# Clustered attention and a channel MLP on one core: block transposes moved from TensorE to VectorE and DMA gathers

## The chip, the cores and the metric

The kernel runs on 1 core of one Trainium2 chip. The metric is the time of one execution on the device, in microseconds (us). Engines are named as in the profile: PE is TensorE, DVE is VectorE, ACT is ScalarE, POOL is GpSimd, SP is the engine whose queue issues nearly all DMAs.

## The reference, cut to what matters

```python
# q, k, v: (4 batches, 8 heads, 768 tokens, 64), centroids: (8, 16, 64)
q_assign = argmax(q_n @ c_n.T); k_assign = argmax(k_n @ c_n.T)      # q_n, k_n, c_n: rows divided by their norms
mask = q_assign[:, :, :, None] == k_assign[:, :, None, :]
scores = where(mask, 0.125 * q @ k.T, -1e9)
attn = softmax(scores);  x = (attn @ v) laid out as (4, 768, 512)
u = x + (x.T @ U @ V).T             # U: (768, 32), V: (32, 768), mixing over tokens
out = u + relu(u @ w_ch1) @ w_ch2   # (512, 2048), (2048, 512)
```

The argmax does not change when a token's similarities are all scaled, so q and k are not normalised in the kernel; only the centroids are.

## The kernel before

**Attention.** The work is cut into 16 pairs of heads (`i`, 4 to a batch). A pair takes 12 score tiles of 128 keys by 2 times 384 queries (`scores`, L474 and L476), their exponentials on ACT (`pr`, L479), their running sum on POOL (`T`, L489) and the products with v in two bursts (`values`, L497, tile `o_ps`). Before the exponentials it needs the largest score of each query: 24 matmuls into PSUM banks (`rowmax`, L450, tile `ps_max`), each read by a DVE reduction (L452). These banks come from a pool of four, `work`, which most other PSUM tiles of the stage share.

**Clusters.** The mask is part of the score matmuls: one-hot rows of the clusters are placed among the rows of q and k (`X1[...][64:96]`), scaled by 2^60. `sims` multiplies tokens with centroids and ACT scales the result by the centroids' norms (L343). `largest` turns the similarities with three PE transposes (L350, tile `ps_simT`), so that tokens lie on partitions. Five DVE operations (L354 to L366) find the first largest cluster and write one-hots. `clusters_T` turns those with six bf16 PE transposes (L375, tile `ps_oh`), ACT scales them (L377), and four DMAs put them in place.

**Mix.** At the end of each batch `mix_u`, `mix_sum` and `mix_v` compute u from x. u goes to DRAM (`u_scr`).

**MLP.** Batch 0 is multiplied in two halves of 384 tokens with 16 steps each (`gemm1`, `gemm2`); meanwhile the weights of batches 1 to 3 are prepared in blocks (`recover`, `combine`, `split_high`, `split_low`) and stored to DRAM (`store_block`, `store_sum`, tensors `wc`). Batches 1 to 3 use a two-level scheme of seven block products instead of eight ("sevens": `seven1`, `seven2`), 16 steps of seven products a batch, with weights fetched from `wc` on SP's queue (`fetch_w1`, `fetch_w2`). They need u with channels on partitions: `fetch_half` reads 384 tokens of u into `st`, `turn_half` turns them with 12 PE transposes (L766) and four ACT copies (L767). `u_sums` (L779, on DVE) and `u_halves` then prepare the operands.

**Order.** The program is one straight list. Every call is put on it by `at(time, ...)`: a unit of time is one score tile in attention (12 a pair), one step in batch 0's MLP, and four sevens products behind it. The tables `times`, `mixes`, `stages` and numbers in the loops set it, the list is sorted, and each engine runs its instructions strictly in that order, SP its DMAs too.

Of the kernel before, what the change touches and what calls it, by code (L numbers as in the profile page):

```python
# [35 lines left out]
ALU = mybir.AluOpType  # L36
# [17 lines left out]
GV = 6  # L54
BIG = float(2.0 ** 60)
# [16 lines left out]
    "place_ones":      (-14.55, -12.25,  -6.11,   None,   None, -20.84),
    "load_v":          ( -19.2,  -5.08,  -7.21,   None, -22.04,  -9.26),
    "rowmax":          (-14.88, -14.94,  -14.8, -12.52,  -8.11, -11.77),
    "rowmax_T":        ( -3.08,  -3.31,  -3.73,  -3.18,   0.25,  -2.19),
    "rowmax_place":    ( -2.26,  -2.27,   -2.6,   0.84,    2.2,  -0.15),
    "scores":          (     0,  -0.97,  -0.37,  -0.47,   0.82,   0.95),
    "weights":         (  1.45,  -0.22,   0.44,   2.06,   3.14,   1.67),
    "values":          (  1.31,   1.51,   0.02,   1.05,   3.05,   1.39),
    "sums":            ( 14.31,  14.69,  13.43,  14.01,  15.51,  15.47),  # L80
    "sums_T":          ( 16.16,  15.81,   14.3,  15.86,  17.06,  16.44),
    "normalise0":      ( 18.83,  16.88,  14.88,  19.57,  20.85,  21.01),
    "normalise1":      ( 21.59,  17.72,  15.28,   26.3,  23.84,  20.15),
    "largest":         (-23.05, -22.46, -20.21,   None,   None, -21.05),
    "clusters":        ( -21.3, -22.24, -20.12,   None,   None, -18.18),
# [4 lines left out]
    "mix_u":    ( 18.88,  18.35,  18.48,  16.57),  # L90
    "mix_sum":  ( 19.11,   19.1,  19.15,  17.65),
    "mix_v":    (  20.5,   20.4,  20.68,  18.42),
# [5 lines left out]
    "g0":   ( 35.66,  38.22,  42.54,  52.94),  # L98
    "g1":   (-26.11, -21.73,  -20.5, -18.29),
    "g2":   (  -2.6,  -1.45,  -0.45,  -0.02,   0.0,   0.53),  # L100
# [3 lines left out]
spots = [0.66, -0.06, 1.8, 2.25, 1.26, 2.09, 2.97, 3, 3.49, 3.81, 4.58, 5.03]  # L104
# [13 lines left out]
def clustered_attention_moe(ctx: ExitStack, tc: tile.TileContext, qk, v, cen, moe_U, moe_V, w1, w2, out):  # L118
# [25 lines left out]
    u_scr = [dram.tile([P, NT, DM], F32, name=f"u_scr{b}") for b in range(B)]  # L144
# [89 lines left out]
    for c in range(C):  # L234
        nc.gpsimd.memset(rank[:, c:c + 1], float(C - c))
    ident_b = one.tile([P, P], BF16, name="ident_b")
    osc = one.tile([P, 1], F32, name="osc")
    obi = one.tile([P, 1], F32, name="obi")
    sel = late.tile([P, 32], F32, name="sel")

    rep = late.tile([P, 96], F32, name="rep")
    onehot = [one.tile([P, NT, 4, 32], BF16, name=f"oh_{i}") for i in range(2)]
    ones = one.tile([2 * NT, P], F32R, name="ones")

    def constants(k):
        if k == 0:
            nc.gpsimd.memset(ones.bitcast(F32), 1.0)
            nc.gpsimd.memset(onehot[0], 0.0)
            make_identity(nc, ident_b)
            for k in range(4):  # L250
                nc.gpsimd.memset(osc[32 * k:32 * k + 32], (1.0, BIG)[k % 2])
                nc.gpsimd.memset(obi[32 * k:32 * k + 32], (0.0, -BIG)[k % 2])
        else:
            nc.gpsimd.memset(onehot[1], 0.0)
# [14 lines left out]
    def table(f):  # L269

        nc.scalar.activation(warm, rank[:, 0:1], f)
# [4 lines left out]
    def turn_centroids(p):  # L276
# [59 lines left out]
    def sims(i):  # L336
# [5 lines left out]
        sm = live["sims", i] = sb.tile([P, HS], F32, name="sims", bufs=1)  # L342
        nc.scalar.mul(sm, ps[:, 0:HS], c_rn[:, i % NP:i % NP + 1])  # L343

    def largest(i):

        ps = work("ps_simT")
        sm = live.pop(("sims", i))
# [3 lines left out]
        eq = live["eq", i] = ps[:, 0:HS].rearrange("p (g c) -> p g c", c=C)  # L352
        mx = sb.tile([P, NG4], F32, name="mx")
        nc.vector.reduce_max(mx, eq, axis=AX.X)  # L354
# [812 lines left out]
```

## Time and profile before

| | |
|---|---|
| time, median of 3 runs | 981.08 us (980.56 to 981.95) |
| profiled execution | 982.48 us, its span 980.70 us |
| busy in the span | PE 946.5, DVE 701.1, ACT 472.5, POOL 611.7 us |
| stages in the span (first instructions of each) | start 0, first score tile 31.9, batch 0's MLP about 482, sevens about 611 |

The time of an execution holds the span and what lies around it, here 1.78 us. The busy time of an engine is the union of its instructions; those of PE are pipelined, so a matmul's own duration is longer than the time until the next can start. Where a row below tells of two instructions that follow each other on PE, the difference of their starts is what the first one cost.

### The profile page before, as it was taken

The numbers are of one execution on the slowest core, as the hardware profiler recorded it, in microseconds if no ns is written. First come the engines' busy times: TensorE is split into PE (matmuls) and PEld (weight loads), VectorE is DVE, ScalarE is ACT, GpSimd is POOL, SyncE is SP. The second block draws the span as 40 slices with busy tenths as digits, with TensorE's granted clock in tenths as the row PEclk, the third lists the DMA queues.
The fourth block names the chain that finished last, engine by engine and source line by source line (L and its number), as shares of the span: only waits on it lengthen the run. The fifth ranks groups of instructions, "written<-read, shape, count | busy, mean of one in ns | idle before, by whom it ended". The sixth has DMA issues, their size and how long they took to land.

```text
span 980.7 us, 15364 instructions
## 1 busy us (share of the span) xinstructions
PE 946.5 (97%) x5368; PEld 776.7 (79%) x5368; DVE 701.1 (71%) x1300; ACT 472.5 (48%) x837; POOL 611.7 (62%) x459
## 2 busy tenths in 40 slices
PE   6899999999999999989999999999999999999997
PEld 3566666676667666655788998999999999999997
DVE  5797777877787776686877525856588665986776
ACT  4454555565565554466556554544345333353330
POOL 5456586788778886774255876744286542865433
PEclk9799999999999999999999999999999999999999
DMA  7755454755656663536599896787668686677644
GB/s 182 188 142 130 119 151 119 212 153 146 163 156 185 160 153 76 178 103 203 171 304 342 277 351 263 252 331 264 239 223 302 259 309 258 223 281 276 240 140 150
DMA packets 76158, 205.28 MB, mean 209 GB/s; under 512 B 8561, under 2 KB 42865, under 8 KB 71217
## 3 DMA queue, kind: packets, MB, share of 16 engines
q1 hardware_dynamic: 75552, 203.42, 64.7%
q8 instruction: 42, 0.69, 0.3%
q10 hardware_dynamic: 528, 0.89, 0.3%
q14 instruction: 36, 0.29, 0.1%
HBM read 131.07 MB, written 41.94 MB: 176 GB/s over the span
## 4 chain that ended last, share of the span: by engine, by line
PE 81%; DVE 9%; DMA 4%; ACT 3%; issue 2%; POOL 1%; SPq 0%; DVEq 0%; ACTq 0%; POOLq 0%
PE o_ps L497 13%; PE ps_max L450 8%; PE st L474 6%; PE st L476 6%; PE ps_p L825 3%; PE ps_p L824 3%; PE ps_p L823 3%; PE ps_q L899 3%; PE ps_q L824 3%; PE ps_q L825 3%; PE ps_q L823 3%; PE ps_q L901 3%; PE ps_q L900 3%; PE ps_p L899 2%; PE ps_p L901 2%; PE ps_p L900 2%
## 5 line engine op out<-in xcount | busy, mean ns | idle before, releaser
L489 POOL TENSOR_TENSOR T<-T,pr 128x768 f32<-128x768 f32 x120 | 226.3, 1886 | 47.4 <-ACT pr L479 20.9
L452 DVE TENSOR_REDUCE m<-ps_max 128x1 f32<-128x384 f32 x384 | 195.3, 547 | 84.1 <-PE ps_max L450 82.6
L479 ACT ACTIVATE pr<-st 128x768 f32<-128x768 f32 x192 | 154.9, 813 | 85.9 <-PE st L476 58.6
L497 PE MATMUL o_ps<-pr,vt 128*64 128x384 f32 x768 | 133.5, 498 | 0.1
L450 PE MATMUL ps_max<-arena 128*128 128x384 f32 x384 | 127.4, 382 | 6.5 <-DVE oh L366 2.5
L474 PE MATMUL st<-arena 128*128 128x384 f32 x384 | 105.7, 356 | 1.8 <-ACT pr L479 1.8
L450 PEld LDWEIGHTS ps_max<-arena 128*128 128x128 f32 x384 | 71.2, 194 | 44.9 <-issue 22.0
L497 PEld LDWEIGHTS o_ps<-pr,vt 128*64 128x64 f32 x768 | 53.1, 139 | 67.5 <-issue 61.4
L476 PE MATMUL st<-arena 97*128 97x384 f32 x384 | 100.2, 342 | 3.6 <-issue 1.9
L489 POOL TENSOR_TENSOR T<-pr 128x768 f32<-128x768 f32 x30 | 56.6, 1886 | 63.8 <-ACT pr L479 63.8
L474 PEld LDWEIGHTS st<-arena 128*128 128x128 f32 x384 | 66.7, 191 | 17.0 <-issue 9.9
L476 PEld LDWEIGHTS st<-arena 97*128 97x128 f32 x384 | 70.8, 191 | 5.6 <-issue 4.1
L501 ACT COPY os<-o_ps 128x384 f32<-128x384 f32 x32 | 15.4, 480 | 106.0 <-PE o_ps L497 106.0
L824 PE MATMUL ps_p<-arena,w 128*128 128x384 f32 x186 | 62.2, 334 | 0.0
L823 PE MATMUL ps_p<-arena,w 128*128 128x384 f32 x186 | 62.2, 334 | 0.0
L825 PE MATMUL ps_p<-arena,w 128*128 128x384 f32 x186 | 62.2, 334 | 0.0
L823 PE MATMUL ps_q<-arena,w 128*128 128x384 f32 x150 | 50.1, 334 | 0.0
L824 PE MATMUL ps_q<-arena,w 128*128 128x384 f32 x150 | 50.1, 334 | 0.0
L825 PE MATMUL ps_q<-arena,w 128*128 128x384 f32 x150 | 50.1, 334 | 0.0
L390 POOL TENSOR_TENSOR arena<-R,arena 128x768 fp32r<-128x768 f32 x18 | 34.3, 1908 | 13.8 <-ACT arena L385 8.2
L824 PEld LDWEIGHTS ps_p<-arena,w 128*128 128x128 f32 x186 | 34.9, 188 | 0.1
L823 PEld LDWEIGHTS ps_p<-arena,w 128*128 128x128 f32 x186 | 34.9, 188 | 0.1
(538 smaller groups left out, 2387.4 us busy)
## 6 DMA issues: line engine op xcount, KB each, us to landing
w<-wc SPq DMA_DIRECT2D x24, 1024.0 KB
w<-wc SPq DMA_DIRECT2D x24, 768.0 KB
arena<-wc SPq DMA_DIRECT2D x20, 768.0 KB
rw<-in_w SPq DMA_DIRECT2D x27, 512.0 KB
R<-in_qk SPq DMA_DIRECT2D x32, 384.0 KB
arena<-arena SPq DMA_DIRECT2D x32, 384.0 KB
arena<-arena SPq DMA_DIRECT2D x64, 192.0 KB
wc<-f SPq DMA_DIRECT2D x46, 256.0 KB
```

The lines of the kernel that those rows point to most:

```text
L450: nc.tensor.matmul(ps[:, 0:HS], x1[:, 0, g // 2, g % 2, t * P:(t + 1) * P], x1[:, 1, h, g % 2, :], start=True, stop=True)
L452: nc.vector.reduce_max(live["m2", i][:, h, u:u + 1], ps[:, 0:HS], axis=AX.X)
L474: nc.tensor.matmul(st[:, j, 0:HS], x1[:, 1, hk, j, ks], x1[:, 0, h, j, :], start=True, stop=False)
L476: nc.tensor.matmul(st[:, j, 0:HS], x2[0:97, 1, hk, j, ks], x2[0:97, 0, h, j, :], start=False, stop=True)
L479: nc.scalar.activation(pr, st[:, :, 0:HS], AF.Exp, scale=SCALE)
L489: eng.tensor_add(T, live["p", i, h, 0] if c == 1 else T, live["p", i, h, c])
L497: nc.tensor.matmul(o_ps[64 * j:64 * j + 64, 0:HS], vv[:, c, j, :], pr[:, j, :], start=(c == 0), stop=(c == NT - 1))
L823: nc.tensor.matmul(ps, w[:, 0, k], u[:, 0, k], start=(k == 0), stop=False)
L824: nc.tensor.matmul(ps, w[:, 0, k], u[:, 1, k], start=False, stop=False)
L825: nc.tensor.matmul(ps, w[:, 1, k], u[:, 0, k], start=False, stop=(k == 1))
L899: nc.tensor.matmul(ps, w[:, 0], h[:, 0], start=(j == 0), stop=False)
L900: nc.tensor.matmul(ps, w[:, 0], h[:, 1], start=False, stop=False)
```

## The change

Four things change, and with them most numbers of the tables.

1. **Similarities and one-hots** are turned by DVE in blocks of 32 by 32 (`nc.vector.transpose`, a STREAM_TRANSPOSE in the rows): the similarities in place in their PSUM bank, the one-hots from SBUF to SBUF. The norms are multiplied into the centroids at the start, so that ACT no longer scales the similarities (but for pair 0) nor the one-hots. `clusters` is now eight calls, 0.7 units apart, and holds one `work` bank from `sims` to its sixth call.
2. **u of batches 1 to 3** is turned in blocks by DVE and stored so that DMAs can gather it with channels on partitions: batches 1 and 2 in `mix_v`, batch 3 during batch 1's sevens (`fetch_half`, `turn_blocks`, `store_half`). `fetch_columns` is 16 DMAs a batch, each of 32 partitions times 24 runs of 32 floats, 128 bytes a run.
3. **mix_u** puts its second round on 256 columns instead of 512, and **mix_sum** multiplies two fp32r halves of xu instead of one fp32 xu. The second half is a DVE subtraction.
4. **Times**: `values` puts its six calls 0.03 instead of 0.001 units apart, and many numbers move by hundredths up to a few units.

```diff
-        sm = live["sims", i] = sb.tile([P, HS], F32, name="sims", bufs=1)
-        nc.scalar.mul(sm, ps[:, 0:HS], c_rn[:, i % NP:i % NP + 1])
-
-    def largest(i):
-            nc.tensor.transpose(ps[:, t * P:(t + 1) * P], sm[:, t * P:(t + 1) * P], ident)
-    def clusters_T(i):
-            nc.tensor.transpose(ps[:, t * P:(t + 1) * P], onehot[i % 2][:, tile_of(t)], ident_b)
-        nc.scalar.activation(live["ohT", i], ps[:, 0:S], AF.Identity, scale=osc, bias=obi)
+        live["eq", i] = live["sims", i] = ps[:, 0:HS]
+        if i == 0:
+            sm = live["sims", i] = sb.tile([P, HS], F32, name="sims", bufs=1)
+            nc.scalar.mul(sm, ps[:, 0:HS], c_rn[:, 0:1])
+
+    def clusters(i, k):
+        if k == 0:
+            nc.vector.transpose(live["eq", i], live.pop(("sims", i)))
+            return
...
+            nc.vector.tensor_tensor(out=onehot[:, :, t, 0:C], in0=eq, in1=most, op=(ALU.subtract, ALU.is_equal)[t])
+        else:
+            ohT = live["ohT", i] = sb.tile([P, S], F32, name="ohT", bufs=1)
+            nc.vector.transpose(ohT.rearrange("p (t b r) -> p b t r", t=2, b=NB), onehot)
...
-        for t in range(NT):
-            g = t % 4
-            nc.tensor.matmul(ps[32 * g:32 * g + 32, :], u_w[:, t, :], x[:, t, :],
-                             start=(t < 4), stop=(t + 4 >= NT))
+        for t in range(4):
+            nc.tensor.matmul(ps[32 * t:32 * t + 32, :], u_w[:, t, :], x[:, t, :], start=True, stop=False)
+        for g in range(4):
+            t, cols = 4 + g // 2, slice(256 * (g % 2), 256 * (g % 2) + 256)
+            nc.tensor.matmul(ps[32 * g:32 * g + 32, cols], u_w[:, t, :], x[:, t, cols], start=False, stop=True)
+        nc.scalar.copy(hi, ps)
+        nc.vector.tensor_sub(lo, ps, hi)
...
-        nc.vector.tensor_add(x[:, t, :], ps, x[:, t, :])
+        y = x[:, t, :] if b % 3 == 0 else ps
+        nc.vector.tensor_add(y, ps, x[:, t, :])
+        if b % 3:
+            nc.vector.transpose(x[:, t, :], ps)
+    def store_blocks(b, t, x):
+        for a in range(4):
+            nc.sync.dma_start(out=u_blk[b][:, t:t + x.shape[1], a, :], in_=x[32 * a:32 * a + 32])
...
-    def turn_half(b, h, d):
-        ps = work("ps_uT")[:, 0:HS] if b == 1 else bank()
-        for t in range(HT):
-            nc.tensor.transpose(ps[:, t * P:(t + 1) * P], pool["st"][:, t, d * P:(d + 1) * P], ident)
-        nc.scalar.copy(pool["ys"][1 - b % 2][:, d, h], ps)
+    def fetch_columns(b, k, d):
+        y = pool["ys"][1 - b % 2][32 * k:32 * k + 32, d].rearrange("p h (n c) -> p (h n) c", c=32)
+        x = u_blk[b].rearrange("r t a (d k c) -> d k r (t a) c", d=ND, k=4)[d, k]
+        nc.sync.dma_start(out=y, in_=x)
...
-        c = M0 + (2.8, 6.8, 10.8, 14.8, 17.5, 20.0, 22.7, 26.4)[n_]
+        c = M0 + (2.68, 6.65, 10.8, 14.8, 17.5, 20.06, 22.7, 26.81)[n_]
-                at(c + 0.3 * r, recover, n_, k, g, r)
+                at(c + 0.57 * r, recover, n_, k, g, r)
```

The first place is DVE's order in a pair in the middle of attention (`m` are row maxima, `ps_simT` the turned similarities, `ps_sim` the similarities in their bank, `oh` the one-hots, `rv` the reciprocal sums). Before:

```order
L452 TENSOR_REDUCE m_2389<-ps_max 128x1 x4
L354 TENSOR_REDUCE mx<-ps_simT 128x24
L355 TENSOR_TENSOR ps_simT<-ps_simT,mx 128x384
L452 TENSOR_REDUCE m_2389<-ps_max 128x1 x2
L362 TENSOR_TENSOR ps_simT<-ps_simT,rank 128x384
L363 TENSOR_REDUCE ps_simT<-ps_simT 128x24
L366 TENSOR_TENSOR oh_128<-ps_simT,rank 128x24x16
L452 TENSOR_REDUCE m_2389<-ps_max 128x1 x2
```

The same place on DVE now:

```order
L345 STREAM_TRANSPOSE ps_sim<-ps_sim 128x384
L377 TENSOR_TENSOR arena<-R,arena 128x768
L351 TENSOR_REDUCE most<-ps_sim 128x24
L423 TENSOR_REDUCE m_1987<-ps_max 128x1 x3
L355 TENSOR_TENSOR ps_sim<-ps_sim,most 128x384
...
L361 TENSOR_TENSOR oh<-ps_sim,most 128x12x16
L490 TENSOR_SCALAR rv<-ps_sumT 128x12
L492 RECIPROCAL rv<-rv 128x12
L361 TENSOR_TENSOR oh<-ps_sim,most 128x12x16
L423 TENSOR_REDUCE m_1987<-ps_max 128x1 x3
L364 STREAM_TRANSPOSE ohT<-oh 128x12x2x32
```

Five operations in two groups have become eight, two of them transposes, spread singly among the row maxima.

The second place is SP's queue near the end of batch 0's MLP (`wc` are the stored weight blocks, `w` the first weights of the sevens, `f` the buffer that u of batch 1 goes to). Before:

```order
L705 DMA wc_0_98<-f 256x1x256
L706 DMA wc_0_98<-rw 256x1x256
L794 DMA w_93<-wc_0_94 128x2048
L794 DMA w_93<-wc_0_94 128x1536
L705 DMA wc_1_95<-f 256x1x256
L706 DMA wc_1_95<-f 256x1x256
```

The same place on SP now:

```order
L761 DMA f<-u_blk_91 32x24x32 x2
L693 DMA wc_0_99<-f 256x1x256
L694 DMA wc_0_99<-rw 256x1x256
L761 DMA f<-u_blk_91 32x24x32 x2
L788 DMA w_94<-wc_0_95 128x2048
L788 DMA w_94<-wc_0_95 128x1536
L761 DMA f<-u_blk_91 32x24x32 x6
L693 DMA wc_1_96<-f 256x1x256
L694 DMA wc_1_96<-f 256x1x256
```

Fourteen of batch 1's sixteen gathers now stand ahead of the stores of the seventh weight block (the first four of them a few rows above the piece); the two reads of u that stood further up in this stage are gone.

The third place is PE's order in the sevens (`ps_p` and `ps_q` are their PSUM banks, `st` the half of u). Before:

```order
L901 MATMUL ps_q<-hx_5010,arena 128x384
L766 MATMUL ps_p<-ident,st 128x128 x3
L899 MATMUL ps_q<-arena 128x384
L900 MATMUL ps_q<-arena 128x384
L901 MATMUL ps_q<-arena 128x384
```

Now no row of PE reads `st`; the products follow each other without the eight groups of three transposes that a batch had.

## Rows read from the trace of the kernel before

**Rows 1.** The page: the span, and busy time of the engines.
```profile
span 980.7 us, 15364 instructions
PE 946.5 (97%) x5368; PEld 776.7 (79%) x5368; DVE 701.1 (71%) x1300; ACT 472.5 (48%) x837; POOL 611.7 (62%) x459
```
**Rows 2.** Windows: length, busy time of PE, PEld, DVE, ACT, POOL, granted clock, DMA share, GB/s.
```profile
200.00:250.00 50.00, 49.24 (x306) 34.48 (x300) 37.30 (x76) 28.54 (x43) 43.95 (x25) 1.00 0.62 162
482.00:611.00 129.00, 128.82 (x658) 113.43 (x658) 77.63 (x120) 69.64 (x135) 85.60 (x67) 1.00 0.87 299
611.00:720.00 109.00, 108.19 (x627) 106.94 (x626) 73.99 (x142) 48.36 (x104) 51.76 (x50) 1.00 0.72 259
```
**Rows 3.** Timeline of PE in one pair: start, length, engine, line, operation.
```profile
229.56 0.49 PE L350 MATMUL ps_simT<-ident,sims 128*128 128x128 f32 x3
229.80 0.59 PE L474 MATMUL st<-arena 128*128 128x384 f32 x2
...
234.89 0.51 PE L375 MATMUL ps_oh<-ident_b,oh 128*128 128x128 bf16 x6
235.24 0.44 PE L450 MATMUL ps_max<-arena 128*128 128x384 f32 x1
```
**Rows 4.** Timeline of PE in the mix of batch 1.
```profile
267.69 1.91 PE L543 MATMUL ps_xu<-xt,u_w 128*32 128x512 f32 x12
269.53 0.61 PE L450 MATMUL ps_max<-arena 128*128 128x384 f32 x2
...
270.69 1.02 PE L550 MATMUL ps_rep<-xu,rep 128*96 128x512 f32 x2
271.64 0.85 PE L340 MATMUL ps_sim<-R,cT 128*32 128x384 f32 x8
...
273.60 0.40 PE L559 MATMUL ps_h<-x,v 96*128 96x512 f32 x1
273.83 0.52 PE L474 MATMUL st<-arena 128*128 128x384 f32 x2
```
**Rows 5.** Timeline of PE in batch 1's sevens.
```profile
664.90 0.49 PE L766 MATMUL ps_p<-ident,st 128*128 128x128 f32 x3
665.15 0.42 PE L899 MATMUL ps_q<-h,arena 128*128 128x384 f32 x1
```
**Rows 6.** Groups by line and shape: busy, mean ns, idle before and its releasers.
```profile
L766 PE MATMUL ps_q<-ident,st 128*128 128x128 f32 x12 | 2.2, 291 | 1.6 <-DVE u L881 1.2 <-DVE h L881 0.4
```
**Rows 7.** Timeline of the start: first row maxima, first score tile.
```profile
17.67 5.66 DVE L452 TENSOR_REDUCE m<-ps_max 128x1 f32<-128x384 f32 x12
...
31.91 0.84 PE L474 MATMUL st<-arena 128*128 128x384 f32 x2
```
**Rows 8.** Groups by line and shape on DVE.
```profile
L560 DVE TENSOR_TENSOR xt<-ps_h,xt 128x512 f32<-128x512 f32 x24 | 16.4, 684 | 6.1 <-PE ps_h L559 5.8
...
L355 DVE TENSOR_TENSOR ps_simT<-ps_simT,mx 128x384 f32<-128x384 f32 x16 | 9.1, 566 | 0.6
...
L489 DVE TENSOR_TENSOR T<-pr 128x768 f32<-128x768 f32 x2 | 1.9, 948 | 0.0
```
**Rows 9.** Line 450: what PE and its weight loads waited for (us, times).
```profile
  DVE m L452: 12.6, 40
```
**Rows 10.** DMA queues from 410 to 420 us: packets, MB, share of 16 engines.
```profile
q10 hardware_dynamic: 24, 0.01, 0.3%
```
**Rows 11.** DMA queues from 555 to 577 us.
```profile
q1 hardware_dynamic: 6803, 7.10, 94.9%
q10 hardware_dynamic: 144, 0.79, 10.0%
```
**Rows 12.** Issues of `wc` DMAs on SP: least, median, largest ns; first and last start.
```profile
L794 SPq DMA_DIRECT2D w<-wc x48: 319/320/628, 577.7 to 922.5; - x48
L706 SPq DMA_DIRECT2D wc<-f x28: 512/570/1152, 494.2 to 640.1; - x28
```
**Rows 13.** Timeline of DVE at the last weight block's recovery.
```profile
593.36 0.69 DVE L681 TENSOR_TENSOR f<-ps_r,arena 128x512 f32<-128x512 f32 x1 [1.89 <-DMA wc<-f]
```

More of the change, by code (lines that the diff above doesn't have):

```diff
@@ L86 @@
+    "clusters":        (-23.85, -22.92,  -23.10,   None,   None, -19.44),
 }
 mixes = {
-    "mix_u":    ( 18.88,  18.35,  18.48,  16.57),
-    "mix_sum":  ( 19.11,   19.1,  19.15,  17.65),
-    "mix_v":    (  20.5,   20.4,  20.68,  18.42),
+    "mix_u":    ( 18.88,  18.35,  18.56,  16.57),
+    "mix_sum":  ( 19.29,   18.76,  19.15,  17.65),
+    "mix_v":    (  20.55,   19.49,  21.51,  18.25),
+    "store_u":  ( 26.55,  26.40,  26.68,  20.55),
 }
@@ L143, in clustered_attention_moe @@
     make_identity(nc, ident)
-    u_scr = [dram.tile([P, NT, DM], F32, name=f"u_scr{b}") for b in range(B)]
+    u_scr = [dram.tile([P, NT, DM], F32, name=f"u_scr{b}") for b in (0, B - 1)]
+    u_blk = [None, *(dram.tile([32, NT, 4, DM], F32, name=f"u_blk{b}") for b in range(1, B))]
     def fetch(srcs, n, queue=nc.sync, rw=None):
@@ L234, in clustered_attention_moe @@
     for c in range(C):
[L235 to L238, printed above, removed]
+        nc.gpsimd.memset(rank[:, c:c + 1], (C - c) * BIG)
     sel = late.tile([P, 32], F32, name="sel")
-    rep = late.tile([P, 96], F32, name="rep")
-    onehot = [one.tile([P, NT, 4, 32], BF16, name=f"oh_{i}") for i in range(2)]
+    rep = late.tile([P, 96], F32R, name="rep")
+    onehot = one.tile([P, NB, 2, 32], F32, name="oh")
     ones = one.tile([2 * NT, P], F32R, name="ones")
@@ L247, in constants @@
             nc.gpsimd.memset(ones.bitcast(F32), 1.0)
[L248 to L252, printed above, removed]
+            nc.gpsimd.memset(onehot, 0.0)
         else:
-            nc.gpsimd.memset(onehot[1], 0.0)
             nc.gpsimd.memset(sel, 0.0)
@@ new lines, in clusters @@
+    def clusters(i, k):
+        if k == 0:
+            nc.vector.transpose(live["eq", i], live.pop(("sims", i)))
+            return
+        eq = live["eq", i].rearrange("p (g c) -> p g c", c=C)
+        ranks = rank.unsqueeze(1).broadcast_to([P, NG4, C])
+        if k in (1, 4):
+            live["most", i] = sb.tile([P, NG4], F32, name="most")
+            nc.vector.reduce_max(live["most", i], eq, axis=AX.X)
+            return
+        most = live["most", i].unsqueeze(2).broadcast_to([P, NG4, C])
+        if k == 2:
+            nc.vector.tensor_tensor(out=eq, in0=eq, in1=most, op=ALU.is_equal)
+        elif k == 3:
+            nc.vector.tensor_tensor(out=eq, in0=eq, in1=ranks, op=ALU.mult)
+        elif k < 7:
+            t = k - 5
+            eq, most = (x.rearrange("p (b t) c -> p b t c", t=2)[:, :, t] for x in (eq, most))
+            nc.vector.tensor_tensor(out=onehot[:, :, t, 0:C], in0=eq, in1=most, op=(ALU.subtract, ALU.is_equal)[t])
+        else:
+            ohT = live["ohT", i] = sb.tile([P, S], F32, name="ohT", bufs=1)
+            nc.vector.transpose(ohT.rearrange("p (t b r) -> p b t r", t=2, b=NB), onehot)
@@ L1028, in clustered_attention_moe @@
             at(when(f"normalise{h}", i), normalise, i, h)
-    for b, (t_u, t_sum, t_v) in enumerate(zip(*mixes.values())):
+    for b, (t_u, t_sum, t_v, t_store) in enumerate(zip(*mixes.values())):
         o = NS * (NP * b + NP - 1)
@@ L1126, in clustered_attention_moe @@
         if b < B - 1:
[L1127 removed]
+            for j, when_ in enumerate((0.02, 0.79, 6.55, 6.17, 6.45, 6.35, 6.9, 6.75)):
                 at(o + 28 + when_, join_up, b, j)
```

204 lines of the change are left out of this document (92 added, 112 removed).

## The prediction

> **What bounds the kernel now.** I read the page's busy shares first: PE is busy 946.5 of the span's 980.7 us, DVE 71%, POOL 62% [rows 1]. Shares hide stages, so the windows came next. In 50 us of attention PE is busy 49.24, POOL 43.95, DVE 37.30; in batch 0's MLP PE works 128.82 of 129 us, in batch 1's sevens 108.19 of 109, all at a granted clock of 1.00 [rows 2]. So PE is the bound nearly everywhere, and its time is the program's time: what leaves PE's list is gained, unless another engine or a transfer comes too late. The next in line differ by stage: DVE and POOL in attention; the DMA engines at the end of batch 0's MLP, where two queues take 94.9% and 10.0% of them [rows 11].
>
> The sum is made against the profiled execution, 982.48 us (span 980.70 and 1.78 around it). The median of the three runs is 1.40 less, which I take off at the end.
>
> **What leaves PE.** The price of an instruction is the time from its start to the next one's start on PE. Matmuls overlap, so their own lengths (0.49 and 0.51 us beside steps of 0.24 and 0.35) would overstate it.
>
> - Three transposes of similarities: 0.24 us [rows 3]. Of 16 pairs two lie in the start, so 14 × 0.24 = 3.4.
> - Six bf16 transposes of one-hots: 0.35 us [rows 3], 14 × 0.35 = 4.9.
> - Turns of u in the sevens: three transposes 0.25 us [rows 5]. 3 batches × 2 halves × 4 groups = 24 groups, 6.0 us. PE also idled 1.6 us ahead of one form of them [rows 6]; that goes too.
> - mix_u: its rows take 1.84 us [rows 4], two rounds of 512 columns: four tiles of tokens side by side, then two. The second round now spreads two tiles over all four places in 256 columns, so a quarter of the time goes, 0.46 × 4 batches = 1.8.
> - mix_sum: its fp32 product of 512 columns (two rows) takes 0.95 us; two fp32r ones take its place, and one of 512 columns costs 0.23 [rows 4]. 0.95 − 2 × 0.23 = 0.49, × 3 = 1.5 (the fourth mix is hidden in batch 0's MLP).
> - The start: pairs 0 and 1 leave out six operations of the chain between the first row maxima at 17.67 and the first score tile at 31.91 us [rows 7], but the turns on DVE take their place, and products of the norms move ahead of it. Between 0 and 3, I take 1.0.
>
> Sum: 3.4 + 4.9 + 6.0 + 1.6 + 1.8 + 1.5 + 1.0 = 20.2 us.
>
> **What DVE gains.** No row of before has a STREAM_TRANSPOSE. The nearest are plain operations of the same shapes: 566 ns for 128x384 in PSUM, 684 ns for 128x512 from PSUM, 948 ns for 128x768 in SBUF [rows 8]; I price a transpose as such, and twice that as the upper bound. A pair gains 0.57 + 0.95 and some 0.2 for the split one-hot, 1.7 us; 16 pairs 27 us. The mixes gain four subtractions and 12 transposes of 512 columns, 16 × 0.69 = 11; batch 3's blocks six, 4. DVE goes from 701 [rows 1] to about 743 us. In attention a pair is some 25 us (half of the 50 us window), so DVE goes from 37.3 to about 40.7 of 50. It is not full, so below, the cost is nothing. But PE waits on it already: for row maxima 12.6 us, 40 times [rows 9]; the added operations stand singly among these maxima, and a `work` bank that row maxima rotate through is held from the similarities until the one-hots. Were each added operation waited for, it would cost 14 × 1.7 = 24. By queueing, waits go as busy over idle share: 0.746/0.254 becomes 0.814/0.186, times 1.5 would make 12.6 into 19; but most of the moves leave each reduction a different place, and PE has work queued two tiles deep. Nearer to nothing: I take 3 us.
>
> A rule speaks for a larger gain. The Trainium skill, "VectorE: DVE Perf Modes", section "The three transpose paths", gives 390 ns for a 128x128 bf16 transpose on TensorE and 311 ns on VectorE. By it the 72 transposes of u alone would have cost 28 us in place of 6.0, and a similarity block's turn on DVE 0.9 us in place of 0.57. The rows show 0.08 us each in a dense PE queue, and the measurement decides.
>
> **What the transfers gain.** A batch's gathers are 16 DMAs of 32 × 24 runs of 128 bytes: 12,288 packets, 768 for each of 16 engines. No row shows a 128-byte packet. At the bandwidth of the busiest stretch (7.10 MB in 22 us, 20 bytes per ns for one engine) it is 6 ns. Small packets, about 0.4 KB, took 0.003 × 10 us × 16 / 24 = 20 ns [rows 10]. The packets of about 1 KB in that busy stretch took 0.949 × 22 us × 16 / 6803 = 49 ns [rows 11]. I take the 20 of the nearest size: 768 × 20 = 15.4 us of all engines a batch; 4.6 and 37.6 at the ends. What goes are the reads of u into `st`, two of 2.2 us (q10's 10.0% of 22 us) for each of batches 1 and 2; batch 3's still come, and its blocks are stored besides, 4.4. The place decides the cost:
>
> - Batch 1's gathers lie in batch 0's MLP where the DMA engines are full. Fourteen of them stand ahead of the seventh block's stores. The last block's recovery on DVE already waited 1.89 us for such a landing [rows 13], and u_sums is queued behind it on DVE; on u_sums waits the first seven, thus PE. The delay is 14/16 × 15.4 − 4.4 = 9.1 us; the order puts that recovery up to 1.2 units (of some 4 us) later, with 5 us of it usable: 4. SP issues one DMA of 128 packets in 320 ns and of 256 in 570 [rows 12], so 768 packets take about 1.3 to 1.6 us, 14 of them 18 to 22 us: 1 more. I take 5; at 49 ns the delay is 32.9 − 4.4 − 5 + 1 = 24; below, at 6 ns, 0.
> - Batch 2's gathers and batch 3's store lie in batch 1's sevens. There DMA was busy 0.72 × 109 = 78.5 us [rows 2]; with 4.4 and 15.4 it is 98 of about 106. It fits, with little to spare: 1. At 49 ns it is 120.5, over by 14. Batch 3's gathers come in the lighter stage behind: nothing; at 49 ns 4.
> - The store's blocks in `mix_v` are as many bytes as before, in attention, with DMA at 0.62 [rows 2]: nothing. If that cover failed, SP would bring row blocks late and the score tiles would wait.
>
> **Sum:** 20.2 − 3 − 5 − 1 = 11.2. So 982.48 − 11.2 = 971.3, less 1.40: 969.9, I say **970 us**.
>
> **The rivals.**
>
> *All of it comes back (chance 0.20).* DVE's additions fall in its idle time and the gathers are hidden: 982.48 − 20.2 − 1.4 = 960.9, and if waits for row maxima shrink because PE's list is looser, a few less: 956 to 963.5. For it: DVE has a quarter of attention idle, and transfers have a whole stage to land. Against: full DMA engines at the end of batch 0's MLP.
>
> *DVE becomes a second bound in attention (0.18).* If a STREAM_TRANSPOSE costs twice the plain operation, a pair gains 3.2 us: 43.7 of 50, the idle quarter becomes an eighth. Waits of 12.6 us go as the inverse of it, to 24: 12 more in place of 3. 969.9 + 9 = 979; 975 to 983. For it: the waits for row maxima that are there. Against: POOL, at 88%, and not DVE is the fuller engine there.
>
> *Slower: packets of 128 bytes are dear (0.15).* At 49 ns each, as the large ones took in the full stretch, batch 1's gathers hold up the last recovery by 24 us, batch 2's cost 14 and batch 3's 4 in place of 6: 969.9 − 6 + 42 = 1006. Each ns costs 0.67 us for batch 1 (14/16 × 768) and, from 30 ns on, 0.77 for batch 2. So the gain is gone near 34 ns: 0.67 × 14 = 9.4 for batch 1 and 0.77 × 4 = 3 for batch 2, together the 11.2 and a little. For it: that the DMA engines are full just there. Against: the small packets of the quiet stretch took 20. The Trainium skill, "DMA: Bandwidth & Descriptors", section "Specifications", says that a transfer under 512 bytes is below line rate, since the engine reads, modifies and writes. No row here shows it; doubling the 20 ns of the quiet stretch, as a second pass for each packet would, gives 40 ns: 13.4 more for batch 1, 0.77 × 10 − 1 = 6.7 for batch 2, a time of 990.
>
> *Likeliest (0.47):* 963.5 to 975.
>
> **How the numbers follow.** The forecast is the likeliest's 970. The all-returns case reaches to 956, the DVE case to 983, and slower packets beyond. With the range from 956 to 985 I leave out most of the dear packets (0.12) and the two ends (0.05). A change under 0.2%, 1.96 us (979.1 to 983.0), is about what three runs cannot tell from none. Faster: 0.47 + 0.20 + two thirds of 0.18 = 0.79. Same: the last third, 0.06. Slower: 0.15.
>
> **What would show it.** Right: PE's steps from a score tile to a row maximum follow on without the pieces of 0.24, 0.35 and 0.25 us; waits of PE for row maxima from DVE stay under some 16 us; the last recoveries on DVE wait several us for their `wc` block to land; u_sums waits for `f` from u_blk; the windows of the gathers show DMA shares near 1 with packets of some 20 ns mean. Wrong: a transpose on DVE of over 1 us for 384 columns with PE idle for row maxima, a queue of gathers with packets at 40 ns or more and PE idle at the start of the sevens, weights of the sevens (`w`) waited for in batch 1, or SP's issue of the gathers so long that the stores and fetches behind it are late.

## The result and the profile after

| | before | changed |
|---|---|---|
| time, median of 4 runs | 981.52 us (980.56 to 982.19) | 964.57 us (963.39 to 966.88) |
| profiled execution | 982.48 us, span 980.7 | 963.78 us, span 962.0 |

The ratio is 0.9831, with a 95% interval of 0.9809 to 0.9853: 17 us faster. The prediction was 970, within 956 to 985; it forecast 11.2 us, and the direction, size and range held. Its terms did not: several were off, in opposite directions. The windows by stage show first where.

The page of the changed kernel, for [rows 1]:

```profile
span 962.0 us, 14997 instructions
PE 920.9 (96%) x5151; PEld 756.8 (79%) x5151; DVE 737.7 (77%) x1368; ACT 443.7 (46%) x787; POOL 605.9 (63%) x448
```

PE lost 25.6 us of busy time, the span only 18.7. The windows of three stages, with the columns of [rows 2]: attention from the first score tile to batch 0's first product, batch 0's MLP, and the sevens to the end. First the kernel before:

```profile
31.90:467.70 435.80, 423.37 (x2485) 282.86 (x2484) 324.92 (x625) 240.97 (x357) 321.64 (x175) 0.98 0.56 151
467.70:610.70 143.00, 142.82 (x739) 125.64 (x738) 89.02 (x140) 78.14 (x151) 87.17 (x68) 1.00 0.84 289
610.70:980.70 370.00, 360.33 (x2074) 356.95 (x2072) 266.23 (x486) 142.13 (x306) 189.68 (x163) 0.99 0.68 248
```

The same stages of the changed kernel:

```profile
31.60:459.50 427.90, 409.36 (x2366) 272.27 (x2365) 351.39 (x681) 221.29 (x328) 319.74 (x175) 1.00 0.57 153
459.50:598.70 139.20, 139.20 (x719) 123.66 (x718) 89.22 (x142) 74.92 (x143) 83.32 (x65) 1.00 0.92 296
598.70:962.00 363.30, 354.46 (x2026) 352.42 (x2024) 273.39 (x492) 136.76 (x290) 191.07 (x166) 1.00 0.77 263
```

The start gave 0.3 us, attention 7.9, batch 0's MLP 3.8, the sevens 6.7. The stages in which I expected transfers to cost gave the most for what left them. In attention PE's idle time rose from 12.4 to 18.5 us (length less busy). Waits of PE in the changed kernel's attention that the kernel with u turned by PE (run 2 below) does not have, from its timeline (last: idle time before, and what ended it):

```profile
262.74 0.50 PE L535 MATMUL ps_h<-x,v 96*128 96x512 f32 x1 [0.35 <-DVE xt L539]
265.01 0.50 PE L535 MATMUL ps_h<-x,v 96*128 96x512 f32 x1 [0.49 <-DVE xt L539]
267.36 0.44 PE L421 MATMUL ps_max<-arena 128*128 128x384 f32 x1 [0.44 <-DVE xt L539]
...
292.86 0.66 PE L421 MATMUL ps_max<-arena 128*128 128x384 f32 x1 [1.91 <-issue]
...
403.66 0.41 PE L421 MATMUL ps_max<-arena 128*128 128x384 f32 x1 [2.34 <-DMA arena<-ohT]
408.75 0.59 PE L447 MATMUL st<-arena 97*128 97x384 f32 x2 [1.27 <-DMA arena<-mT]
```

They stand in two groups, each once for batch 1 and once for batch 2 (the first group's waits of batch 2, near 375 us, are not shown): in and behind the mix, where DVE turns u (L539), and 10 to 30 us later, where DMAs of one-hots (`ohT`) and of row maxima (`mT`) land late. For the wait at 292.86 the trace names no releaser (`issue`); at the same place run 5 below names the DMA of `ohT`. The prediction had no wait for the turns in the mix (its 3 us for DVE were for row maxima), and it put the stores at nothing.

The prices of the turns on DVE, for [rows 8]:

```profile
L364 DVE STREAM_TRANSPOSE ohT<-oh 128x768 f32<-128x768 f32 x16 | 15.5, 967 | 0.1
L345 DVE STREAM_TRANSPOSE ps_sim<-ps_sim 128x384 f32<-128x384 f32 x15 | 8.8, 586 | 1.9 <-PE ps_sim L335 1.9
L539 DVE STREAM_TRANSPOSE xt<-ps_h 128x512 f32<-128x512 f32 x12 | 8.6, 717 | 0.4
```

586, 717 and 967 ns, against the 566, 684 and 948 assumed: within 5%, a turn costs what a plain operation of its shape costs.

A gather's packets can be read where nothing else runs: the half microsecond from 794.5 us of the changed kernel (queue: packets, MB, share of 16 engines).

```profile
q1 hardware_dynamic: 842, 0.11, 136.5%
```

842 packets of 128 bytes in 0.5 us are 0.5 × 16 / 842 = 9.5 ns a packet of one engine (the share passes 100%, so packets overlap; by it one takes 13 ns). I took 20. A batch's gathers are 768 × 9.5 = 7.3 us of all engines, not 15.4.

### The profile page after: what moved, and what is told of

Read it like the earlier page. It is cut to its first block, busy times and chain, and to the rows that moved or that the text cites. A ratio compares the mean times of both kernels' runs of the same rounds, so it can differ in the third digit from the quotient of the medians.

```text
span 962.0 us, 14997 instructions
## 1 busy us (share of the span) xinstructions
PE 920.9 (96%) x5151; PEld 756.8 (79%) x5151; DVE 737.7 (77%) x1368; ACT 443.7 (46%) x787; POOL 605.9 (63%) x448
## 4 chain that ended last, share of the span: by engine, by line
PE 84%; DVE 9%; DMA 4%; ACT 2%; issue 1%; SPq 0%; DVEq 0%; ACTq 0%
PE o_ps L468 13%; PE ps_max L421 7%; PE st L445 6%; PE st L447 5%; DVE m L423 3%; PE ps_p L817 3%; PE ps_p L819 3%; PE ps_p L818 3%; PE ps_q L893 3%; PE ps_q L895 3%; PE ps_q L894 3%; PE ps_q L818 3%; PE ps_q L817 3%; PE ps_q L819 3%; PE ps_h L596 2%; PE ps_p L893 2%
## 5 line engine op out<-in xcount | busy, mean ns | idle before, releaser
L460 POOL TENSOR_TENSOR T<-T,pr 128x768 f32<-128x768 f32 x120 | 223.4, 1862 | 46.0 <-ACT pr L450 17.1
L421 PE MATMUL ps_max<-arena 128*128 128x384 f32 x384 | 124.7, 388 | 13.8 <-DVE m L423 4.0
L472 ACT COPY os<-o_ps 128x384 f32<-128x384 f32 x32 | 15.4, 481 | 92.4 <-PE o_ps L468 92.4
L377 POOL TENSOR_TENSOR arena<-R,arena 128x768 fp32r<-128x768 f32 x18 | 36.7, 2044 | 18.2 <-ACT arena L372 12.5
L605 DVE SCALAR_TENSOR_TENSOR hx<-ps_h,hx 128x384 fp32r<-128x384 f32 x32 | 17.6, 550 | 25.4 <-ACT hx L604 25.3
L817 PEld LDWEIGHTS ps_p<-arena,w 128*128 128x128 f32 x186 | 34.9, 188 | 1.3 <-DVE f L913 1.2
```

Of the source, the lines that this page charges most:

```text
L377: eng.tensor_sub(part(X2[i % 3], 0, h), live["R", i][:, 2 * h:2 * h + 2].rearrange("p j q -> p (j q)"), part(X1[i % 3], 0, h))
L421: nc.tensor.matmul(ps[:, 0:HS], x1[:, 0, g // 2, g % 2, t * P:(t + 1) * P], x1[:, 1, h, g % 2, :], start=True, stop=True)
L460: eng.tensor_add(T, live["p", i, h, 0] if c == 1 else T, live["p", i, h, c])
L817: nc.tensor.matmul(ps, w[:, 0, k], u[:, 0, k], start=(k == 0), stop=False)
```

## The experiments

All ratios are to the kernel before, timed beside on the same chip (its medians there 981.0 to 981.8 us). "Run 1" to "run 10" are the numbers of the paragraphs below.

| kernel | median us | ratio (95%) |
|---|---|---|
| changed | 964.57 | 0.9831 (0.9809 to 0.9853) |
| changed, again | 964.49 | 0.9823 (0.9809 to 0.9837) |
| the mix alone | 981.25 | 0.9998 (0.9986 to 1.0011) |
| u turned by PE | 958.82 | 0.9768 (0.9753 to 0.9784) |
| bank free early | 965.65 | 0.9839 (0.9817 to 0.9860) |
| gathers twice | 974.63 | 0.9934 (0.9917 to 0.9952) |
| no turns in the mix | 958.79 | 0.9766 (0.9743 to 0.9789) |
| u by PE, stores in blocks | 967.06 | 0.9849 (0.9837 to 0.9862) |
| batch 3 in blocks | 954.31 | 0.9717 (0.9705 to 0.9730) |
| batches 2 and 3 in blocks | 953.84 | 0.9722 (0.9708 to 0.9736) |
| row maxima placed earlier | 977.53 | 0.9964 (0.9949 to 0.9978) |
| one-hots placed first | 965.72 | 0.9853 (0.9834 to 0.9871) |
| similarities turned thrice | 967.85 | 0.9867 (0.9853 to 0.9881) |

**1. The mix alone.** The kernel before with the new `mix_u` and `mix_sum`.

```diff
-        for t in range(NT):
-            g = t % 4
-            nc.tensor.matmul(ps[32 * g:32 * g + 32, :], u_w[:, t, :], x[:, t, :],
-                             start=(t < 4), stop=(t + 4 >= NT))
+        for g in range(4):
+            t, cols = 4 + g // 2, slice(256 * (g % 2), 256 * (g % 2) + 256)
...
+        nc.vector.tensor_sub(lo, ps, hi)
```

> The kernel before with the third part of the change alone (mix_u's second round in 256 columns, mix_sum as two fp32r products; no number of the tables is moved). By the sum: 1.8 + 1.5 = 3.3 us less, 0.9966 of the time before, since PE is the bound. The rival, that a large part of the 17 us comes from moved numbers and from stretches of low granted clock that the new order avoids: no fixed sign, between 3 us faster and 3 us slower, with another pattern of low clock in the trace.

No difference that can be measured; the 3.3 us of the sum lie outside the interval. In the profiled execution PE's idle time in attention is 14.7 us against 12.4, with a new wait of 1.40 us behind the mix of batch 1 for a weight conversion on DVE (`rw_t`). That the added subtraction stands in front of it would fit, but no run isolates it.

**2. u turned by PE.** The changed kernel with its second part undone.

```diff
-        for d in range(ND):
-            for k in range(4):
-                at(o - (10 if b == 1 else 15) + 1.07 * d + 0.51 * k, fetch_columns, b, k, d)
...
+        if b == 1:
+            fetched, turns = (o - 13.9, o - 9.5), (o - 11.5, o - 7.4)
+        else:
+            fetched, turns = (o - 20, o - 14), (o - 15.7, o - 8.7)
+        for h in range(2):
+            at(fetched[h], fetch_half, b, h)
+            for d in range(ND):
+                at(turns[h] + 0.4 * d, turn_half, b, h, d)
```

> The changed kernel with its second part undone: u of batches 1 to 3 goes to DRAM row by row, is read in halves and turned by PE at the times of before; no turns in mix_v, no gathers. Theory: gathers are hidden and cost nothing, the turns on DVE cost the 4.3 us that PE waited for xt of mix_v. So PE's 6.0 us and the 1.6 us of waits come back and 4.3 go: 964.6 + 3.3 = about 968, 1.003 to 1.004 of the changed kernel. Rival 1, that the mix waits are only moved from elsewhere: the full 7.6, about 972. Rival 2, that gathers cost what the prediction put down (6 us): 964.6 + 7.6 - 6 - 4.3, about 962, faster than the changed kernel.

958.8: faster than the changed kernel, so its second part loses 5.7 us. The time alone is nearest to the rival of the dear gathers. The windows speak against it:

```profile
31.80:446.80 415.00, 405.25 (x2366) 271.40 (x2364) 342.30 (x669) 220.72 (x328) 320.39 (x175) 1.00 0.58 157
446.80:588.20 141.40, 141.40 (x742) 125.98 (x741) 89.36 (x142) 77.99 (x151) 85.66 (x67) 1.00 0.87 294
588.20:956.70 368.50, 360.37 (x2074) 356.96 (x2072) 268.29 (x486) 143.29 (x306) 188.86 (x164) 0.99 0.69 249
```

Against the changed kernel, batch 0's MLP and the sevens are 2.2 and 5.2 us longer, as they should be with PE's turns back, and the gathers cost nothing there but 1.4 us of waits for weights in batch 1's sevens. But attention is 12.9 us shorter, 415.0 against 427.9. The loss lies where the turns and the stores in blocks are made, not where the gathers run.

**3. The bank free early.** The sum goes to SBUF and is turned there.

```diff
-        y = x[:, t, :] if b % 3 == 0 else ps
-        nc.vector.tensor_add(y, ps, x[:, t, :])
+        nc.vector.tensor_add(x[:, t, :], ps, x[:, t, :])
         if b % 3:
-            nc.vector.transpose(x[:, t, :], ps)
+            nc.vector.transpose(x[:, t, :], x[:, t, :])
```

> The changed kernel, where mix_v of batches 1 and 2 writes its sum into x in SBUF and turns it there in place, so that the PSUM bank is free after the sum (0.69 us) and not after sum and turn (1.4 us). DVE's work is the same. Theory, that PE's 4.3 us of waits for xt come from the bank being held: 2 to 4 us faster, 961 to 963, and the waits for xt of mix_v nearly gone. Rival, that DVE's time itself is what is late: within 1 us of the changed kernel, with the waits moved to the row maxima.

The rival's result in the time, 1.1 us from the changed kernel. The waits for `xt` are gone, and waits for row maxima stand in their place (0.66, 0.77, 0.74 and 0.49 us behind the two mixes). This profile alone would leave a doubt: PE's idle time in attention is 16.5 us, less than the changed kernel's 18.5, and three stretches at half the granted clock, 3.4 us each, may have taken the gain back. Run 5 below settles it, since it is this kernel less its 12 turns and nothing else: 958.79 against 965.65. With the bank free early in both, 8.5 us of DVE cost 6.9 us. It is DVE's time that is late, not the bank.

**4. Gathers twice.**

```diff
         nc.sync.dma_start(out=y, in_=x)
+        if b == 1:
+            nc.sync.dma_start(out=again[d, k], in_=x)
```

> The changed kernel, where each of batch 1's 16 gathers is issued a second time, the same runs of 128 bytes into a scratch tensor in DRAM that nobody reads: 12,288 more packets in the stage whose DMA engines are full. At the 9.6 ns a packet that the trace of the changed kernel shows in stretches of gathers alone (about 213 GB/s) that is 7.4 us more of all engines, and some 10 us of SP's issue. Theory, that the stage has slack behind its transfers: 0 to 2 us slower. Rival, the prediction's way of counting, by which a transfer in that stage delays the first seven by its own length less 5 us at most: the slack was used up by the first set, so 6 to 8 us slower, 971 to 973.

10 us slower, more than the rival's 6 to 8. PE stood once, for ACT's half of a step, and its granted clock was 0.5 for 10 us from 3 us into that wait on; first its timeline, then windows:

```profile
592.22 0.80 PE L616 MATMUL y<-arena,hx 128*128 128x512 f32 x1 [8.76 <-ACT hx L605]
```

```profile
586.00:598.00 12.00, 5.78 (x17) 4.49 (x17) 5.51 (x10) 3.40 (x7) 0.00 (x0) 0.57 1.02 259
598.00:609.00 11.00, 11.00 (x56) 9.87 (x56) 7.03 (x9) 6.17 (x13) 10.01 (x8) 1.00 1.00 414
```

ACT waited for the recovery of the last weight block on DVE, and that for its block. SP's first store of the seventh block and that recovery, in the changed kernel and then here:

```profile
577.30 0.59 SPq L693 DMA_DIRECT2D wc<-f  x1
580.88 0.69 DVE L669 TENSOR_TENSOR f<-ps_r,arena 128x512 f32<-128x512 f32 x1 [3.87 <-DMA wc<-f]
```

```profile
586.87 0.59 SPq L694 DMA_DIRECT2D wc<-f  x1
590.43 0.69 DVE L670 TENSOR_TENSOR f<-ps_r,arena 128x512 f32<-128x512 f32 x1 [14.14 <-DMA wc<-f]
```

So the mechanism that the prediction feared, a late recovery of the last block, is real in this stage, but PE stood for ACT in batch 0's MLP and not for `u_sums` and the first seven. The store leaves SP 9.6 us later and the recovery starts 9.6 us later: what delays it is SP's time in front of the store, 24.0 us for the 28 gathers there and 13.2 for the 14 of the changed kernel. Most hold SP for 0.6 to 1.4 us, one for 4.0; whether the long ones wait for full engines, no run separates. One set of gathers left slack; a second used it up.

**5 and 6. Turns and stores apart.** Run 5 is the changed kernel without the turns:

```diff
-        y = x[:, t, :] if b % 3 == 0 else ps
-        nc.vector.tensor_add(y, ps, x[:, t, :])
-        if b % 3:
-            nc.vector.transpose(x[:, t, :], ps)
+        nc.vector.tensor_add(x[:, t, :], ps, x[:, t, :])
```

Run 6 is the kernel of run 2 with `store_u` of the changed kernel, and reads to match:

```diff
-        nc.sync.dma_start(out=u_scr[b], in_=x)
+        if b % 3:
+            store_blocks(b, 0, x)
...
+            for a in range(4):
+                nc.sync.dma_start(out=pool["st"][32 * a:32 * a + 32], in_=u_blk[b][:, h * HT:(h + 1) * HT, a, :])
```

> The changed kernel without the 12 turns of DVE in mix_v (it leaves them out, so u of batches 1 and 2 reaches the MLP unturned); the sums, the stores in blocks and the gathers stay. With u turned by PE instead, attention took 415.0 us against 427.8 (from the first score tile to the first product of batch 0's MLP). Theory: these 8.6 us of DVE, placed where DVE has row maxima, the mix and the normalisation to do, make up that difference: attention 415 to 418 us, the time 952 to 955. Rival: the stores in blocks, four DMAs a batch in front of the one-hots' DMAs on SP, are what is late: attention 425 to 428, the time 963 to 965.

> The kernel with u turned by PE, where u of batches 1 and 2 is stored in four DMAs in the blocks' layout, as in the changed kernel, and read back by four DMAs a half. Theory (the turns on DVE cost the time in attention): 958 to 960, attention within 1 us of 415. Rival (the stores in blocks cost it): attention 424 to 428, the time 967 to 971.

Both costs exist. Without the turns the time is 5.8 us less than the changed kernel's (its runs spread from 954.4 to 962.4), and the waits for `ohT` (2.07 and 2.33 us) stay. With the stores in blocks alone the time is 8.2 us more than run 2's. How the 12.9 us of attention divide is less sure. Up to the end of attention these two kernels issue the same instructions in the same order on every engine, and yet their profiles have 420.1 us (run 5, its shortest execution) and 424.4 (run 6, its longest, with two stretches of 3.4 us at half the granted clock). So the stores cost 5.0 to 9.4 us of attention, and the turns the other 3.4 to 7.8. Run 6 has the gaps in question, with no turn of u on DVE:

```profile
292.62 0.47 PE L421 MATMUL ps_max<-arena 128*128 128x384 f32 x1 [3.12 <-issue]
```

```profile
400.51 0.41 PE L421 MATMUL ps_max<-arena 128*128 128x384 f32 x1 [2.04 <-DMA arena<-ohT]
```

SP's queue shows what stands in front of the one-hots. The changed kernel, batch 1 (start, length, line, transfer):

```profile
276.01 5.47 SPq L550 DMA_DIRECT2D u_blk<-xt  x4
281.58 3.86 SPq L228 DMA_DIRECT2D arena<-arena  x2
285.49 0.60 SPq L641 DMA_DIRECT2D wc<-w  x1
286.13 2.95 SPq L228 DMA_DIRECT2D arena<-arena  x2
289.18 2.59 SPq L228 DMA_DIRECT2D arena<-ohT  x4
```

The same rows with the store in one piece, run 2:

```profile
273.47 1.78 SPq L540 DMA_DIRECT2D u_scr<-xt  x1
275.34 2.42 SPq L228 DMA_DIRECT2D arena<-arena  x2
277.81 1.30 SPq L635 DMA_DIRECT2D wc<-w  x1
279.22 4.13 SPq L228 DMA_DIRECT2D arena<-arena  x2
283.40 2.80 SPq L228 DMA_DIRECT2D arena<-ohT  x4
```

Four DMAs hold SP for 5.47 us, one for 1.78; the one-hots leave 5.8 us later, of which 2.5 are there when the store starts (276.01 against 273.47) and 3.2 come behind it. The store's bytes are the same. But the engines move less in that time, with other transfers among them. The queue's rows for 12 us from the store on, in the changed kernel (276 to 288 us) and then in run 2 (273 to 285):

```profile
q1 hardware_dynamic: 1273, 2.85, 97.0%
```

```profile
q1 hardware_dynamic: 870, 3.59, 99.0%
```

Full engines both times, with 2.2 KB a packet on average in one and 4.1 in the other, and 2.85 MB moved instead of 3.59.

**7. One-hots placed first.** To see whether SP's order is enough.

```diff
-    "place_clusters":  (-18.26, -15.82, -15.03,   None, -10.24, -12.43),
+    "place_clusters":  (-18.26, -17.90, -15.03,   None, -10.24, -12.43),
```

> The changed kernel with one number moved: the four DMAs of the one-hots of each batch's fourth pair stand on SP ahead of two placements of queries, not behind them. In the changed kernel the one-hots were ready at 285.75 us, but SP, held 5.47 us by the four stores in blocks, issued them from 289.18; PE then stood 1.91 us and its granted clock was 0.5 for 4 us. Theory (the stores cost by SP's queue in front of the one-hots): one-hots some 3 us earlier there, the gaps of 1.9 and 2.3 us gone and the low clock with them, 3 to 6 us faster than the changed kernel, 0.977 to 0.980 of before. Rival (the stores cost by what they move, or the placements that now stand behind are as urgent): within 1 us of the changed kernel.

> The changed kernel once more, on the same chip as the other runs of this group. 963 to 967 us; the gaps at about 291 and 401 us in the same places.

My theory fell. The one-hots of batch 1's mix left SP 1.2 us after they were ready (288.64, 289.82) instead of 3.4, yet PE went on at 295.24 only, behind a wait of 1.41; the wait at about 402 stayed (2.54). One of 1.46 came at 78.7: the two placements that now stand behind the one-hots left SP at 77.3 in batch 0 and not at 68.1, so this wait is most likely the move's own, as the rival had it. SP's order is not enough. What remains is that the transfers themselves are slow on full engines, or that the placements are as urgent; no run separates these, nor the number of DMAs.

The changed kernel's second profile showed no low clock in attention, but idle time of 20.2 us in place of 18.5, and the same length within 0.2.

**8. Row maxima placed earlier**, in the kernel before.

```diff
-    "rowmax_place":    ( -2.26,  -2.27,   -2.6,   0.84,    2.2,  -0.15),
+    "rowmax_place":    ( -2.26,  -2.27,  -2.82,   0.84,    2.2,  -0.15),
```

> The kernel before with one number moved: the negated row maxima of the last pair go to ACT ahead of a weight conversion and not behind it, 0.68 us earlier, and their DMA with them. In the trace of before PE waited 1.89 us at 437.4 us for that row and its granted clock was 0.5 for 8 us behind it. Theory, that low clock there follows from this wait and that it is part of what the change gained: the wait shrinks to about 1.2 us, and the time is 0.7 us less if the clock falls all the same, some 4 us less (0.996) if it doesn't. Rival, that the clock has nothing to do with the wait: the time as before, the clock low at the same place.

4 us faster in the median (2 to 5 by the interval), from one weight conversion of ACT that now stands behind two rows and not ahead of them; nothing else in the order of any engine differs. The profiled execution is the longest of its runs, and in it attention is 433.4 us for 435.8, so it shows 2.4 us of the 4. The timeline of PE before had this:

```profile
436.79 0.62 PE L474 MATMUL st<-arena 128*128 128x384 f32 x2 [1.43 <-ACT pr L479]
439.30 0.98 PE L476 MATMUL st<-arena 97*128 97x384 f32 x2 [1.89 <-issue]
```

Its windows there, up to, in and behind the low clock:

```profile
93.00:437.00 344.00, 337.75 (x2030) 228.47 (x2027) 254.31 (x501) 190.22 (x279) 268.81 (x147) 1.00 0.56 149
437.00:445.00 8.00, 6.11 (x22) 2.53 (x23) 5.33 (x7) 2.45 (x4) 4.93 (x3) 0.57 0.76 248
445.00:467.00 22.00, 20.81 (x128) 13.24 (x126) 17.08 (x25) 15.29 (x26) 9.28 (x6) 1.00 0.56 185
```

And with the number moved:

```profile
437.00:442.00 5.00, 4.62 (x18) 2.31 (x20) 4.90 (x7) 2.91 (x5) 4.84 (x3) 0.66 0.57 147
442.00:465.00 23.00, 21.84 (x135) 13.61 (x131) 18.63 (x27) 15.29 (x26) 10.05 (x7) 1.00 0.73 239
```

The wait of 1.89 us is gone altogether, and not only shorter. The low clock still begins behind the wait of 1.43 us that stands ahead of it (1.36 here), but lasts 3.4 us and not 6.8. So the theory holds for its length and not for its start; why it starts is open, since the changed kernel has a wait of 1.30 us at the same place and no low clock.

**9. Similarities turned thrice**, in the first kernel of run 10 (batch 3 in blocks, 954.3 us): the same result, 28 turns more.

```diff
-            nc.vector.transpose(live["eq", i], live.pop(("sims", i)))
+            for _ in range(3 if i > 1 else 1):
+                nc.vector.transpose(live["eq", i], live["sims", i])
```

> The kernel with batch 3's u alone turned in blocks (954.3 us), where the similarities of 14 pairs are turned in place three times and not once, with the same result: 2 x 0.59 x 14 = 16.4 us more of DVE in attention, spread over the pairs. Theory: such single operations among row maxima mostly fit into DVE's idle quarter, the cost is 0 to 5 us. Rival, DVE as a second bound in attention: each added us of DVE costs about one, as the 8.6 us in mix_v did: 12 to 16 us, 966 to 970.

The rival's result: 13.5 us for 28 × 0.595 = 16.7 us of DVE, 0.8 us for each. In its profile PE's idle time in attention is 20.0 us for 10.0, with 8.3 us of waits for row maxima for 3.0; behind two of these waits (1.76 and 1.72 us) the granted clock was 0.5 for 3.4 us each, which is 3.4 us more. Its window of attention:

```profile
31.70:462.40 430.70, 410.69 (x2366) 271.69 (x2364) 362.46 (x697) 220.97 (x328) 319.60 (x175) 0.99 0.56 152
```

DVE's share of attention is 0.746 before, 0.825 in run 2, 0.821 in the changed kernel and 0.842 here. Between the first two DVE took on 17 us and attention still became shorter, since more left PE; from there, DVE's work lengthens it. The share alone is no limit: the changed kernel has a lower one than run 2 and loses by its turns. Here the added turns stand three in a row, in the mix (run 3 against run 5, also 0.8) behind each other.

**10. The better versions.** Only batch 3's u goes through blocks, read, turned, stored and gathered in batch 2's sevens; then batch 2's too, in batch 1's.

```diff
+            for h in range(2):
+                at(o - 28 + (0.5, 6.0)[h], fetch_half, b, h)
+                for t in range(HT):
+                    at(o - 28 + (2.5, 8.0)[h] + 0.5 * t, turn_blocks, t)
+                at(o - 28 + (4.5, 10.0)[h], store_half, b, h)
+            for d in range(ND):
+                for k in range(4):
+                    at(o - 15 + 1.07 * d + 0.51 * k, fetch_columns, b, k, d)
```

> The kernel with u of batches 1 and 2 turned by PE, but batch 3's turned in blocks by DVE and gathered by DMAs, read, turned and stored in the first part of batch 2's sevens. A half of u turned by PE made a half batch of sevens 16.2 us long in place of 14.6, so two halves less: 958.8 - 3.2 = 955.6. Rival: the gathers and the added read and store, 7.4 + 4.4 us of all DMA engines, hold up the weights of the sevens: 958 to 962.

> As the kernel with batch 3's u alone turned in blocks by DVE (954.3 us), and batch 2's u the same way: stored row by row at its mix, read, turned and stored in blocks in the first part of batch 1's sevens, gathered in its second part; batch 1's u stays with PE. Two more halves of PE's turns go, 1.6 us each: 954.3 - 3.2 = 951.1. Rival: batch 1's sevens are fuller of transfers than batch 2's (the changed kernel waited 1.4 us there for weights beside gathers), and here the read and the store of batch 2 come on top: 953 to 956, with waits for arena from wc.

954.3 us, 10 less than the changed kernel, a little more than expected: both halves of PE's turns are gone from batch 2's sevens, and no new wait stands there. With batch 2 as well, 953.8: by the intervals no difference. Batch 1's sevens became shorter by the two halves (14.6 us for 16.2 each), and its profile gives back 0.8 us in the first stretch of sevens (a wait of 0.56 in it) and a wait of 1.44 us at the end. "Half batch" in the two expectations means the two stretches of seven products among which PE turned a half of u.

## Why the prediction held, and what failed in it

The forecast was near because errors cancelled. Without its second part the change gives 22.8 us (run 2), and the second part takes 5.7 back; some 4 of the 22.8 (2 to 5) are what run 8 gets from one moved number, which was no term. By the prediction's steps:

- **What leaves PE: the right work, 2 us too small in attention.** PE's busy time there fell from 423.4 to 405.3 (run 2), 18.1 us. Of this 4.3 stand in the low clock of before at 89 and at 437 us, where the granted clock was 0.5 for 3.4 and 6.8 us with PE busy for 8.5 of them. The other 13.8, of which 0.3 are a shorter slow start, stand against 3.4 + 4.9 and three quarters of 1.8, with 1.5: 11.2. The steps in [rows 3] were read right, but they are not the whole price: behind a group of three, the second product starts 0.26 us after the first, where 0.175 is usual; for the 14 groups of similarities that is 1.2 us more. And **the stretches of low clock were not read**: I took the clock as 1.00 from three windows [rows 2], where the whole of attention has 0.98.
- **Turns of u: 6.0 + 1.6 forecast.** From run 2 to the changed kernel 2.2 + 5.2 and the 1.4 us of new waits make 8.8. A half of u in the sevens lengthened its stretch of seven products from 7.36 to 8.95 us, 0.40 us for each of its four groups and not the 0.25 of [rows 5]. The 1.6 us of waits [rows 6] were all but gone in run 2 already (0.3).
- **The start: 1.0 forecast, 0.3 measured.**
- **The mix: 3.3 forecast.** Alone it gives nothing that can be measured (run 1).
- **DVE: 3 us forecast for row maxima; the turns in the mix had no price of their own, and that failed.** The prices of the operations were right. I read 12.6 us of waits as PE's, spread thinly [rows 9]; that row counts PE's weight loads too, and of PE itself only 0.2 us waited for `m` of the reductions in attention. That the 3 us came about (3.0 in run 2, 3.3 in the changed kernel) is luck, as the row was the wrong one. The 12 turns in the mix come together behind each other, and their 8.5 us cost 6.9 (run 3 against run 5). DVE as a second bound was a rival at 0.18, by twice the price of a turn; where work was added, it came about at the plain price (runs 5 and 9).
- **The store's blocks, put at nothing for equal bytes and DMA at 0.62: wrong**, 8.2 us (run 6). The mean of the window hid a full stretch (97.0% behind the store), and equal bytes were not equal time: four DMAs of 2 KB runs for one with longer ones. The text named row blocks behind SP as what would come late if that cover failed; it was one-hots and row maxima.
- **Gathers: 5 + 1 forecast, 0 + 1.4 measured.** The packet price was 9.5 ns and not 20, so the delay by the prediction's own formula is 7.3 × 14/16 − 4.4 = 2.0 us, under the 5 of slack. The last recovery waited 3.87 us for its block where it had waited 1.89 [rows 13], and nothing came of it. Run 4 shows that SP's time counted for more than the packets: the formula gave SP 1 us, at 18 to 22 us for fourteen gathers. They took 13.2, and fourteen more, which made it 24.0, delayed the recovery by 9.6.

The rival of dear packets is out by the price (9.5 ns, where it needed 34 for no gain). The Trainium skill, "DMA: Bandwidth & Descriptors", section "Specifications", puts transfers under 512 bytes below line rate; the trace agrees: 211 GB/s in the half microsecond of gathers alone, 385 GB/s in 571 to 573 us of the same kernel, where all packets are of 8 KB or more. It was no loss since the stages had the time.

What stays open: how the 8.2 us of the stores in blocks divide between SP's time, the number of DMAs and the shorter runs; why the mix alone gives nothing; and how much of run 2's 22.8 us is due to moved numbers, beyond the one of run 8, since no run has the turns of part 1 without them.

## What to carry to other kernels

DVE, at 75% of attention, took on 17 us in single operations among others with little loss (2.8 us more of waits for row maxima), but each us of turns put behind each other cost 0.8: look at where the work is put together, not only at how much it is. Equal bytes are not equal transfers: when a store is cut into pieces with shorter runs, count SP's time and what is queued behind it, above all small DMAs that PE waits for. A gain can be cancelled inside the same change: taking its parts one by one found a version 10 us better than the whole.

## What the runs showed of the hardware

- A turn of 32 by 32 blocks by DVE, in place in PSUM too, takes within 5% what a plain fp32 operation of its shape takes: 586 ns for 128x384 (566), 717 for 128x512 (684), 967 for 128x768 (948).
- Three fp32 transposes of 128 by 128 in PE's dense queue cost 0.25 us to the next start, and 0.33 to 0.40 with the delay of the products behind.
- Waits of PE of 1.4 to 9 us were followed several times, not always, by a granted clock of 0.5 (1.2 GHz): 3.4 us of it behind a wait of 1.9 us in the changed kernel, 6.8 behind one of 1.4 us before, with one of 1.9 in it, 10 from within one of 8.8 us (run 4); none behind 2.3 us at 401 us in the changed kernel, nor behind 1.6 and 2.3 us in its second profile.
- Gathered 128-byte packets ran at 9.5 ns a packet and engine when alone.
- A gather's DMA of 768 packets held SP for 0.66 us in the median of the changed kernel's 48, 0.55 at least and 3.8 at most.
